# Reordering the transposed loads, the first FFN pass and the output tail of a gated SSM + FFN mix

## The chip, the cores and the metric

The kernel runs on one core of a Trainium2 chip. The metric is the device time of one execution in microseconds (us); lower is better. A core has TensorE (PE in the profile; its weight loads are the row PEld), VectorE (DVE), ScalarE (ACT), GpSimd (POOL) and SyncE (SP), each with an instruction queue of its own that runs in order. Here SP issues nearly all DMAs; ACT issues some at the start.

## The reference

Inputs are bf16; x is 2048 x 448. The result is `g * a + (1 - g) * b`, row by row:

```python
g = sigmoid((x * gate_w).sum(-1, keepdims=True))
# a: a diagonal complex state space model with 448 states
dt = exp(log_dt); Lam_bar = exp(dt * Lam); B_bar = ((Lam_bar - 1) / Lam)[:, None] * (B_re + 1j * B_im)
h[t] = Lam_bar * h[t-1] + B_bar @ x[t]                 # for 2048 steps t
a[t] = 2 * real((C_re + 1j * C_im) @ h[t]) + x[t] * Dskip
# b: a feed-forward network, 448 -> 1792 -> 448
b = silu(x @ w1) @ w2
```

## The kernel before, in words

The program is one function, `gated_mix`. A small class, `Tracker`, keeps for every named buffer who wrote and who read it, and puts semaphore waits in front of each instruction; each engine gets its list in the order in which the function emits it. So the order of the calls in the source is the order of work on every engine, written out by hand.

**Layout.** The 2048 rows are taken as 1024 pairs (`x2` is 1024 x 896: even row, then odd row). `XT` holds x transposed: chunks 0 to 3 are the 448 channels of the even rows, 4 to 7 of the odd rows; three chunks have 128 channels and the last has 64, called the remainder. Halves h = 0, 1 are 512 pairs each. Keys: `XTe00..3` (even, h 0; made by PE transposes), `XTe1` (even, h 1), `XTo0`/`XTr0` and `XTo1`/`XTr1` (odd main chunks / odd remainder of half 0 and 1; all DMA transposes by `ldt`, L221). `XR` holds the remainders once more on the other 64 partitions, copied by `swap_xr` on DVE (L233 for half 1 of the even rows, key `XR1a`; L411 for half 0), so that two matmuls of 64 rows can use the two halves of the PE array side by side. `W1E` is w1, its remainder rows loaded twice, on partitions 0 to 63 (key `W1Ea`) and 64 to 127 (`W1Ez`); `W1Ed` is the larger part of the columns from 896 on. `BT` is B transposed (keys `BT0`, `BT1`; remainders `BT2`, `BT3`), with a DVE copy of the remainder to the other half (L516, key `BTz`) and a packed copy `BR` of 64 re/im columns (L518). `XN` is x as it lies, in two halves `XN0`, `XN1`; `GWB` and `DB` are gate_w and Dskip broadcast to 128 partitions.

**Stages.** `ffn1_first` (L355) and `ffn1(c, ...)` (L326 full chunks, L339 remainders) make the FFN's first product in transposed form for chunk c (c = 0, 1 even halves, 2, 3 odd halves), ACT applies SiLU (L366). `bu(pt, h)` (L660 full chunks, L672 remainders) makes B x for a pair of state blocks; ACT copies it out (L682, L684, L689). Main and remainder matmuls alternate in order (`half`). `scan(pt)` and `scan3()` run the recurrence on DVE: `weigh`, `turn`, `back` and `even` are their steps, `run(gen, n)` emits the next n of them. `gate` (DVE, L585) multiplies `XN` with `GWB`, `gate2` (ACT, L602) sums its rows, `skip` (DVE, L593) multiplies `XN` with `DB`. `ffn2(c, q)` (L629) is the FFN's second product for 128 rows; ACT evicts it with the factor 1 - g (L634). `phases` (POOL, L477 and L479) and `phases2` (DVE, L484) prepare the arguments of the sine tables.

**Output.** 16 tiles of 128 x 448. `yopen` (L828, L830) issues six matmuls of a tile, `yclose` (L841) the two that need the last scan, `yout` (DVE, L851) combines the tile with the gate and the FFN's part into one of 4 buffers of `OT`, and SP stores it (L854). `xg(b)` names places that the gate borrows as scratch: b = 2 is `OT`, b = 3 is `TMPS`.

**Order around the change.** SP issues: x and the weights, `BT0`, `BT1`, `BT2`, `BT3`, `XTo0`, `XTr0`, `XTe1`, `XN0`, `XTo1`, `XTr1`, `XN1`, then W2 and C. PE runs `ffn1_first`, the rest of `ffn1(0)`, `bu(0, 0)`, `bu(3, 0)`, one block of `ffn1(1)`, `bu(0, 1)`, `bu(3, 1)`, the rest of `ffn1(1)`, and on. A block of `ffn1(1)` waits for `XTe1` and `XR1a` before its first matmul; the odd half of `bu(0, 0)` for `XTo0` and `XTr0`, its remainders for all of `BT` and `BTz`; `bu(3, 0)` for `BR`; `bu(0, 1)`, which begins with its remainders, for `XTo1` and `XTr1`.

Of the kernel before, what the change touches and what calls it, by code (L numbers as in the profile page):

```python
# [19 lines left out]
D = 448  # L20
# [126 lines left out]
def gated_mix(nc, A_x, A_Lambda_re, A_Lambda_im, A_B_re, A_B_im, A_C_re, A_C_im, A_log_dt,  # L147
              A_Dskip, B_x, B_w1, B_w2, gate_w, out):
    with ExitStack() as ctx:
        E = ctx.enter_context  # L150
        T = Tracker(nc, ctx)

        def sb(name, shape, dtype):
            return E(nc.sbuf_tensor(name, list(shape), dtype))

        x2 = A_x[0].rearrange("(k i) d -> k (i d)", i=2)
        out2 = out[0].rearrange("(k i) d -> k (i d)", i=2)

# [8 lines left out]
        XR = sb("XR", [128, NK], BF16)  # L167
# [6 lines left out]
        OT = sb("OT", [128, 4, D], BF16)  # L174
# [30 lines left out]
        def xg(b):  # L205
            if b < 2:
                return CO[:, 4 * b:4 * b + 4, :], [f"CO{m}" for m in (range(4) if b == 0 else (1, 4, 5, 6))]
            if b == 2:
                return OT[:, :, :], [f"OT{i}" for i in range(4)]
            v = TMPS[:, :, :].rearrange("p a b -> p (a b)").bitcast(BF16)  # L210
            return v[:, 0:4 * D].rearrange("p (k c) -> p k c", k=4), [f"TMP{i}" for i in range(3)]

        ps = E(nc.psum_tensor("ps", [128, 8, 512], F32))
# [3 lines left out]
        def ld(eng, dst, src, key, group=None):  # L217
            return T.dma(eng, lambda e: e.dma_start(dst, src), writes=[key], group=group)  # L218

        def ldt(dst, src, key, reads=(), group=None, also=()):  # L220
            return T.dma("sp", lambda e: e.dma_start_transpose(dst, src), reads=reads,  # L221
                         writes=[key, *also], group=group)
# [19 lines left out]
        def row(v):  # L242
            return v.rearrange("(o n) -> o n", o=1)
# [5 lines left out]
        for i, eng in enumerate(("sp", "act")):  # L249
            T.dma(eng, lambda e, i=i: e.dma_start(XH[:, 2 * i:2 * i + 2, :], x0[:, 2 * i:2 * i + 2, :]),  # L250
                  writes=COK[i:i + 1])
# [14 lines left out]
        gBT = T.group()  # L266
        for i, src in enumerate((A_B_re, A_B_im)):
            ldt(BT[:, 0:3, i * D:(i + 1) * D], src[:, 0:384], f"BT{i}")
        for i, src in enumerate((A_B_re, A_B_im)):
            ldt(BT[:, 3:4, i * D:(i + 1) * D], src[:, 320:448], f"BT{2 + i}", group=gBT)  # L270

        def ldt_odd(h):
            hs = slice(h * 512, (h + 1) * 512)
            ldt(XT[:, 4:7, hs], x2[hs, 448:832], f"XTo{h}")
            ldt(XT[:, 7:8, hs], x2[hs, 768:896], f"XTr{h}")

        def load_xn(h):
            ld("sp", XN[:, 8 * h * D:8 * (h + 1) * D].rearrange("p (k c) -> p k c", k=4),
               x2[h * 512:(h + 1) * 512, :].rearrange("(k p) c -> p k c", p=128), f"XN{h}")

        for dst, src, key in ((GWB, gate_w, "GW"), (DB, A_Dskip, "DB")):
            ld("act", dst[:, :], row(src).partition_broadcast(128).rearrange("p o n -> p (o n)"), key)
        ldt_odd(0)
        ldt(XT[:, 0:4, 512:1024], x2[512:1024, 0:512], "XTe1")
        load_xn(0)
        ldt_odd(1)
        load_xn(1)
        XC_ALL = ["XC0", "XC1"] + [f"XC3_{q}" for q in range(4)]

        T.op("pool", lambda e: e.memset(ID[:, :], 1.0), writes=["ID"])  # L290
# [4 lines left out]
             writes=["IOTA"])  # L295
# [5 lines left out]


        n_bank = [0]

        def nxt():
            n_bank[0] += 1
            return BANKS[(n_bank[0] - 1) % len(BANKS)]

        half = [False]

        def ffn1_mm(c, fbs):

# [35 lines left out]
        def ffn1_first():  # L348

            banks = [nxt() for _ in range(NFA)]  # L350
            for j in range(4):
                p = slice(0, 128 if j < 3 else 64)

                for fb, bank in enumerate(banks):
                    T.op("pe", lambda pe, fb=fb, bank=bank, j=j, p=p: pe.matmul(  # L355
                        ps[:, bank, :], W1E[p, j, fb * 128:(fb + 1) * 128], XT[p, j, 0:512],
                        start=(j == 0), stop=(j == 3)),
                        reads=[f"W1Ej{j}" if j < 3 else "W1Ea", f"XTe0{j}"], writes=[f"ps{bank}"])
                if j == 0:
                    yield  # L360
            nxt()
            yield list(enumerate(banks))
# [46 lines left out]
        for j in range(4):  # L409
# [9 lines left out]
            reads=["ps7"], writes=["PV"])  # L419
# [12 lines left out]
        def c1(n, pt):  # L432
            i = pc(n)
            return P[:, i, pt:pt + 1]
# [9 lines left out]
        def pact(o, a, f, ra, scale=1.0, bias=0.0):  # L444
# [16 lines left out]
            reads=["f2"] + SGN, writes=["f2s"])  # L461
# [38 lines left out]
        def tmp(m):  # L500
            if m < 4:
# [11 lines left out]
             reads=["li"] + SGN, writes=["lis"])  # L513
# [3 lines left out]
             writes=["BTz"] + BTK[2:4])  # L517
# [293 lines left out]
        n_o = [0]  # L811
# [3 lines left out]
        def state(kt, odd, m):  # L815
            t0 = kt * 128
            return HS[:, m, t0 + H0:t0 + H0 + 128] if odd else VE[:, m, t0:t0 + 128]

        def sk(kt, odd, ms):
            return [f"H{'S' if odd else 'E'}{m}_{kt // 4}" for m in ms]  # L820

        def yopen(kt, odd):
            bank = nxt()

            def mm(pe):
                ins = None
                for m in YA:
                    ins = pe.matmul(ps[:, bank, 0:D], state(kt, odd, m), CO[:, m, :], start=(m == 0), stop=False)  # L828
                tile = 2 * kt + odd
                return pe.matmul(ps[:, bank, 0:D], ID[:, :], XN[:, tile * D:(tile + 1) * D], start=False, stop=False)  # L830
            T.op("pe", mm, reads=sk(kt, odd, YA) + [f"CO{m}" for m in YA] + [f"XD{kt // 2}", "ID"],
                 writes=[f"ps{bank}"])
            return kt, odd, bank

        def yclose(kt, odd, bank):
            tile = 2 * kt + odd

            def mm(pe):
                ins = None
                for m in YB:  # L840
                    ins = pe.matmul(ps[:, bank, 0:D], state(kt, odd, m), CO[:, m, :], start=False, stop=(m == YB[-1]))  # L841
                return ins
            T.op("pe", mm, reads=sk(kt, odd, YB) + [f"CO{m}" for m in YB], writes=[f"ps{bank}"])
            return tile, bank

        def yout(tile, bank):
            kt, odd = tile // 2, tile % 2
            i = n_o[0] % 4
            n_o[0] += 1
            o = OT[:, i, :]  # L850
            T.op("dve", lambda e: e.scalar_tensor_tensor(  # L851
                o, ps[:, bank, 0:D], GT[:, 1, tile:tile + 1], bs(tile), ALU.mult, ALU.add),
                reads=[f"ps{bank}", "GT1", f"BS{tile}"], writes=[f"OT{i}"])
            outs.append(T.dma("sp", lambda e: e.dma_start(  # L854
                out2[kt * 128:(kt + 1) * 128, odd * D:(odd + 1) * D], o),
                reads=[f"OT{i}"], writes=[f"out{tile}"]))
# [7 lines left out]
        def run(g, n=10 ** 9):  # L864
            for _ in range(n):
                if next(g, "end") == "end":
                    break
# [5 lines left out]
        s0, s3, s1, s2 = scan(0), scan3(), scan(1), scan(2, True)  # L873
# [10 lines left out]
        f = ffn1(1)  # L884
# [45 lines left out]
        for q in range(4):  # L930
            ffn2(3, q)
        done = []
        for kt in range(4):
            for odd in (1, 0):
                done.append(yclose(*yopen(kt, odd)))
        run(s2, 1)
        yout(*done.pop(0))
        run(s2, 1)
        while done[2:]:
            yout(*done.pop(0))  # L940
        run(s2, 1)
        while done:
            yout(*done.pop(0))
        opened = [yopen(kt, 1) for kt in range(4, 8)]
        run(s2, 1)
        for kt in range(4, 8):
            opened.append(yopen(kt, 0))
            done.append(yclose(*opened.pop(0)))
        while opened:
            done.append(yclose(*opened.pop(0)))  # L950
        while done:
            yout(*done.pop(0))
        T.wait_all("sp", outs)

        with nc.Block() as block:
# [3 lines left out]
def bass_gated_mix__ssm_conv_s5__dense_activation_silu__prompt_kernel(nc, *args):  # L959
    gated_mix(nc, *args)  # L960
# [28 lines left out]
```

## Time and profile before

| | us |
|---|---|
| median of 3 runs | 151.32 (150.38 to 154.27) |
| the profiled execution | 149.61 |
| its span, first to last instruction | 147.8 |
| PE busy within the span | 139.2 (94%) |
| DVE / ACT / POOL busy | 124.1 / 82.2 / 15.1 |

A timeline row reads: start, duration, engine, line, operation, output<-inputs, shape, how many; a bracket gives the idle time before it and who ended it. "SPq" and "ACTq" are the issuing of DMAs. A row of the DMA view gives the number of issues, the size, and the time from issue to landing. The chain view follows the work that ended last back to the start.

### The profile page before, as it was taken

The page shows a single profiled execution, that of the slowest core. Times are in us where ns is not written, and L with a number is a line of the kernel's source. Part 1 is how long each engine was busy: PE and PEld are TensorE (multiplying, and loading weights), DVE is VectorE, ACT ScalarE, POOL GpSimd, SP SyncE. Part 2 cuts the span into 40 slices and gives each one's busy share as a digit, 9 for nine tenths or more (in the row PEclk, how much of TensorE's full clock was granted, in tenths as well). Part 3 has the DMA queues.
Part 4 walks back from the last instruction along what each step waited for, and adds up shares of the span by engine and source line. Part 5 has one row for each costly group of instructions (what it writes and reads, how often), then busy time and mean ns, then how long its engine had stood idle before and what let it go on. Part 6 is the DMA issues. An engine that isn't in the chain of part 4 may idle for free.

```text
span 147.8 us, 1884 instructions
## 1 busy us (share of the span) xinstructions
PE 139.2 (94%) x715; PEld 63.8 (43%) x715; DVE 124.1 (84%) x164; ACT 82.2 (56%) x130; POOL 15.1 (10%) x20
## 2 busy tenths in 40 slices
PE   6999949799999999999999999999999999999980
PEld 2544313243354543343555343445555555555530
DVE  1673774999999999999999999999999729997372
ACT  1259796868999999995998375471313210000000
POOL 7039990000000000000000000000000000000000
PEclk9999999999999999999999999999999999999997
DMA  4999699999943003003000000000000000211023
GB/s 126 306 248 222 131 164 319 163 381 317 151 102 72 0 0 71 0 0 75 0 0 0 0 0 0 4 0 0 0 0 0 4 0 31 100 55 62 31 93 126
DMA packets 23137, 12.40 MB, mean 84 GB/s; under 512 B 16213, under 2 KB 22617, under 8 KB 23129
## 3 DMA queue, kind: packets, MB, share of 16 engines
q1 hardware_dynamic: 22260, 11.11, 31.8%
q10 hardware_dynamic: 868, 1.18, 3.1%
q8 instruction: 5, 0.08, 0.2%
q14 instruction: 4, 0.02, 0.1%
HBM read 6.26 MB, written 1.84 MB: 55 GB/s over the span
## 4 chain that ended last, share of the span: by engine, by line
PE 62%; ACT 15%; SPq 14%; DMA 5%; issue 2%; DVE 2%; DVEq 0%; ACTq 0%
PE ps L629 21%; PE ps L326 13%; SPq L221 11%; PE ps L828 10%; PE ps L660 8%; DMA XT<-in_A_x_dram 5%; ACT AT L366 3%; PE ps L841 3%; ACT CO L602 3%; PE ps L339 2%; SPq L218 2%; PE ps L830 2%; PE ps L672 2%; DVE OT L851 2%; ACT TMPS L602 2%
## 5 line engine op out<-in xcount | busy, mean ns | idle before, releaser
L629 PE MATMUL ps<-W,AT 128*128 128x448 bf16 x224 | 42.9, 352 | 0.0
L326 PE MATMUL ps<-XT,W1E 128*128 128x512 bf16 x147 | 33.6, 380 | 0.0
L366 ACT ACTIVATE AT<-ps 128x1024 bf16<-128x1024 f32 (+1 forms) x32 | 27.2, 918 | 7.7 <-PE ps L339 7.3
L629 PEld LDWEIGHTS ps<-W,AT 128*128 128x128 bf16 x224 | 21.9, 98 | 20.7 <-ACT AT L366 0.2
L326 PEld LDWEIGHTS ps<-XT,W1E 128*128 128x128 bf16 x147 | 13.7, 98 | 18.9 <-issue 3.0
L660 PE MATMUL ps<-XT,BT 128*128 128x512 bf16 x72 | 16.7, 379 | 1.9 <-issue 1.9
L634 ACT ACTIVATE BT<-ps,GT 128x448 bf16<-128x448 f32 x8 | 5.1, 633 | 15.5 <-PE ps L629 15.5
L851 DVE SCALAR_TENSOR_TENSOR OT<-ps,GT,BT 128x448 bf16<-128x448 f32 x8 | 5.4, 680 | 7.6 <-PE ps L841 7.6
L660 PEld LDWEIGHTS ps<-XT,BT 128*128 128x128 bf16 x72 | 6.7, 98 | 11.1 <-issue 3.7
L730 DVE TENSOR_TENSOR_SCAN G<-P,Q 128x1024 f32<-128x1024 f32 (+1 forms) x6 | 11.3, 1918 | 0.0
L682 ACT ACTIVATE VE<-ps 128x1024 bf16<-128x1024 f32 (+1 forms) x8 | 7.4, 920 | 5.5 <-PE ps L672 4.2
L828 PE MATMUL ps<-CO,HS 128*128 128x448 bf16 x40 | 8.9, 352 | 0.0
L828 PE MATMUL ps<-CO,VE 128*128 128x448 bf16 x40 | 8.9, 352 | 0.0
L696 DVE SCALAR_TENSOR_TENSOR G<-VE,P,HS 128x1024 f32<-128x1024 bf16 (+1 forms) x5 | 7.5, 1494 | 1.6 <-ACT HS L684 1.6
L696 DVE SCALAR_TENSOR_TENSOR HS<-VE,P,G 128x512 bf16<-128x512 bf16 (+1 forms) x10 | 8.1, 856 | 0.2
L684 ACT ACTIVATE HS<-ps 128x1024 bf16<-128x1024 f32 (+1 forms) x8 | 7.4, 921 | 0.8 <-PE ps L660 0.8
L693 DVE TENSOR_TENSOR Q<-G,COS 128x2048 bf16<-128x2048 f32 (+1 forms) x4 | 7.0, 1754 | 0.1
L693 DVE TENSOR_TENSOR Q<-G,SIN 128x2048 bf16<-128x2048 f32 (+1 forms) x4 | 7.0, 1750 | 0.0
L339 PE MATMUL ps<-XT,W1E 64*128 64x512 bf16 x25 | 6.8, 379 | 0.0
L339 PE MATMUL ps<-XR,W1E 64*128 64x512 bf16 x24 | 6.5, 379 | 0.0
L355 PE MATMUL ps<-XT,W1E 128*128 128x512 bf16 (+1 forms) x28 | 6.5, 379 | 0.0
L830 PE MATMUL ps<-XN,ID 128*128 128x448 bf16 x16 | 5.6, 353 | 0.0
(107 smaller groups left out, 181.8 us busy)
## 6 DMA issues: line engine op xcount, KB each, us to landing
XN<-in_A_x_dram SPq DMA_DIRECT2D x2, 896.0 KB, 6.2
out_dram<-OT SPq DMA_DIRECT2D x16, 112.0 KB, 1.7
W<-in_B_w_dram SPq DMA_DIRECT2D x1, 1568.0 KB, 9.0
W1E<-in_B_w_dram ACTq DMA_DIRECT2D x3, 224.0 KB, 6.4
W1E<-in_B_w_dram SPq DMA_DIRECT2D x1, 672.0 KB, 9.2
HS<-HS SPq DMA_DIRECT2D x4, 128.0 KB, 2.4
W1E<-in_B_w_dram SPq DMA_DIRECT2D x2, 224.0 KB, 5.0
CO<-in_A_x_dram SPq DMA_DIRECT2D x1, 256.0 KB, 3.4
```

The costliest lines, as they stand in the source:

```text
L221: return T.dma("sp", lambda e: e.dma_start_transpose(dst, src), reads=reads, writes=[key, *also], group=group)
L326: ins = pe.matmul(ps[:, bank, :], W1E[:, j, fb * 128:(fb + 1) * 128], XT[:, x0 + j, hs], start=(j == 0 and not rf), stop=(j == 2 and rf))
L339: ins = pe.matmul(ps[:, bank, :], W1E[p, 3, fb * 128:(fb + 1) * 128], x, start=rf, stop=not rf)
L366: T.op("act", lambda e: e.activation(a[:, fb:fb + n, :], ps[:, bank:bank + n, :], AF.Silu), reads=[f"ps{bank + i}" for i in range(n)], wri ...
L629: ins = pe.matmul(ps[:, bank, 0:D], a[:, fb, q * 128:(q + 1) * 128], W2[:, fb, :], start=(fb == 0), stop=(fb == NFB - 1))
L660: ins = pe.matmul(ps[:, bank, :], bt(slice(0, 128), j, m), XT[:, 4 * odd + j, hs], start=(j == 0 and not rf), stop=(j == 2 and rf))
L693: T.op("dve", lambda e: e.tensor_tensor(o, a, b, op), reads=reads, writes=writes)
L696: T.op("dve", lambda e: e.scalar_tensor_tensor(o, a, s, b, ALU.mult, ALU.add), reads=reads, writes=writes)
L730: T.op("dve", lambda e, c=c, init=init: e.tensor_tensor_scan(G[:, c, w], rb, Q1[:, c, w], init, ALU.mult, ALU.add), reads=[f"Q1{c}", "rr", ...
L828: ins = pe.matmul(ps[:, bank, 0:D], state(kt, odd, m), CO[:, m, :], start=(m == 0), stop=False)
L830: return pe.matmul(ps[:, bank, 0:D], ID[:, :], XN[:, tile * D:(tile + 1) * D], start=False, stop=False)
L851: T.op("dve", lambda e: e.scalar_tensor_tensor(o, ps[:, bank, 0:D], GT[:, 1, tile:tile + 1], bs(tile), ALU.mult, ALU.add), reads=[f"ps{ban ...
```

## The change

Five edits:

1. **DMA order on SP.** `XTo0` and `XTr0` go ahead of `BT2` and `BT3`; `XTo1` and `XTr1` go ahead of `XN0`; `XN0` and `XN1` come last. The loads of `GWB` and `DB` move from ACT's queue to SP's, between `XTr1` and `XN0`.
2. **`ffn1_first`.** In its last pass (the remainders) every second matmul uses the upper copy: `W1E[64:128]` and `XR` in place of `W1E[0:64]` and `XT`.
3. **Order of the tail.** `turn` of the last scan step comes ahead of the first `yout`, and the first eight tiles are put out two, four and two at a time between `turn`, `back` and `even`. The last eight tiles keep one tile open ahead: open, open, close, open, close, and so on.
4. **Store buffers.** `yout` goes round 8 buffers: 4 in `OT` and 4 in the place of `TMPS`.
5. `half` is set a few lines earlier in the source.

```diff
         for i, src in enumerate((A_B_re, A_B_im)):
             ldt(BT[:, 0:3, i * D:(i + 1) * D], src[:, 0:384], f"BT{i}")
-        for i, src in enumerate((A_B_re, A_B_im)):
-            ldt(BT[:, 3:4, i * D:(i + 1) * D], src[:, 320:448], f"BT{2 + i}", group=gBT)
...
+        ldt_odd(0)
+        for i, src in enumerate((A_B_re, A_B_im)):
+            ldt(BT[:, 3:4, i * D:(i + 1) * D], src[:, 320:448], f"BT{2 + i}", group=gBT)
+        ldt(XT[:, 0:4, 512:1024], x2[512:1024, 0:512], "XTe1")
+        ldt_odd(1)
         for dst, src, key in ((GWB, gate_w, "GW"), (DB, A_Dskip, "DB")):
-            ld("act", dst[:, :], row(src).partition_broadcast(128).rearrange("p o n -> p (o n)"), key)
-        ldt_odd(0)
-        ldt(XT[:, 0:4, 512:1024], x2[512:1024, 0:512], "XTe1")
+            ld("sp", dst[:, :], row(src).partition_broadcast(128).rearrange("p o n -> p (o n)"), key)
         load_xn(0)
-        ldt_odd(1)
         load_xn(1)
...
             for j in range(4):
-                p = slice(0, 128 if j < 3 else 64)
                 for fb, bank in enumerate(banks):
...
+                    up = j == 3 and fb % 2 == 1
+                    p = slice(64, 128) if up else slice(0, 128 if j < 3 else 64)
+                    x = XR[p, 0:512] if up else XT[p, j, 0:512]
...
         def yout(tile, bank):
-            i = n_o[0] % 4
+            i = n_o[0] % 8
             n_o[0] += 1
-            o = OT[:, i, :]
+            o = OT[:, i, :] if i < 4 else xg(3)[0][:, i - 4, :]
...
         for kt in range(4):
             for odd in (1, 0):
                 done.append(yclose(*yopen(kt, odd)))
+        run(s2, 2)
+        flush(2)
         run(s2, 1)
-        yout(*done.pop(0))
+        flush(4)
         run(s2, 1)
-        while done[2:]:
-            yout(*done.pop(0))
-        run(s2, 1)
-        while done:
-            yout(*done.pop(0))
-        opened = [yopen(kt, 1) for kt in range(4, 8)]
-        run(s2, 1)
-        for kt in range(4, 8):
-            opened.append(yopen(kt, 0))
-            done.append(yclose(*opened.pop(0)))
+        flush(8)
+        tiles = [(kt, 1) for kt in range(4, 8)] + [(kt, 0) for kt in range(4, 8)]
+        opened = [yopen(*tiles.pop(0)), yopen(*tiles.pop(0))]
         while opened:
             done.append(yclose(*opened.pop(0)))
-        while done:
-            yout(*done.pop(0))
+            if tiles:
+                opened.append(yopen(*tiles.pop(0)))
+        flush(8)
```

`flush(n)` calls `yout` for up to n closed tiles.

More of the change, by code (lines that the diff above doesn't have):

```diff
@@ L208, in xg @@
             if b == 2:
-                return OT[:, :, :], [f"OT{i}" for i in range(4)]
+                return OT[:, 0:4, :], [f"OT{i}" for i in range(4)]
             v = TMPS[:, :, :].rearrange("p a b -> p (a b)").bitcast(BF16)
@@ L303, in gated_mix @@
         n_bank = [0]
+        half = [False]
         def nxt():
@@ L307, in nxt @@
             return BANKS[(n_bank[0] - 1) % len(BANKS)]
-        half = [False]
         def ffn1_mm(c, fbs):
@@ L351, in ffn1_first @@
             for j in range(4):
-                p = slice(0, 128 if j < 3 else 64)
                 for fb, bank in enumerate(banks):
[L355 to L358, printed above, removed]
+                    up = j == 3 and fb % 2 == 1
+                    p = slice(64, 128) if up else slice(0, 128 if j < 3 else 64)
+                    x = XR[p, 0:512] if up else XT[p, j, 0:512]
+                    T.op("pe", lambda pe, fb=fb, bank=bank, j=j, p=p, x=x: pe.matmul(
+                        ps[:, bank, :], W1E[p, j, fb * 128:(fb + 1) * 128], x, start=(j == 0), stop=(j == 3)),
+                        reads=[f"W1Ej{j}" if j < 3 else "W1Ez" if up else "W1Ea", "XR0a" if up else f"XTe0{j}"],
+                        writes=[f"ps{bank}"])
                 if j == 0:
@@ L847, in yout @@
             kt, odd = tile // 2, tile % 2
-            i = n_o[0] % 4
+            i = n_o[0] % 8
             n_o[0] += 1
-            o = OT[:, i, :]
+            o = OT[:, i, :] if i < 4 else xg(3)[0][:, i - 4, :]
+            extra = xg(3)[1] + ["CT4", "CT5", "CT6"] if n_o[0] == 5 else []
             T.op("dve", lambda e: e.scalar_tensor_tensor(
                 o, ps[:, bank, 0:D], GT[:, 1, tile:tile + 1], bs(tile), ALU.mult, ALU.add),
-                reads=[f"ps{bank}", "GT1", f"BS{tile}"], writes=[f"OT{i}"])
+                reads=[f"ps{bank}", "GT1", f"BS{tile}"], writes=[f"OT{i}"] + extra)
             outs.append(T.dma("sp", lambda e: e.dma_start(
@@ L932, in gated_mix, with flush @@
         done = []
+        def flush(n):
+            for _ in range(n):
+                if done:
+                    yout(*done.pop(0))
         for kt in range(4):
```

## The prediction

> **What bounds the kernel now.** I read the page first, then TensorE's timeline for the places where it stands still, then the queue that feeds it there, then the end.
>
> ```profile
> PE 139.2 (94%) x715; PEld 63.8 (43%) x715; DVE 124.1 (84%) x164; ACT 82.2 (56%) x130; POOL 15.1 (10%) x20
> ```
>
> TensorE is busy for 139.2 us, 94% of the span, so a gain must come out of the other 6%, 8.6 us, or out of shorter TensorE work. Its timeline, where it stops or where an edit touches it:
>
> ```profile
> 18.16 1.46 PE L660 MATMUL ps<-XT,BT 128*128 128x512 bf16 x6
> 21.53 1.46 PE L660 MATMUL ps<-XT,BT 128*128 128x512 bf16 x6 [1.91 <-issue]
> 23.36 0.38 PE L672 MATMUL ps<-XT,BR 64*128 64x512 bf16 x2
> 24.98 2.75 PE L326 MATMUL ps<-XT,W1E 128*128 128x512 bf16 x12
> 27.89 0.38 PE L339 MATMUL ps<-XR,W1E 64*128 64x512 bf16 x1
> 29.18 0.61 PE L672 MATMUL ps<-XT,BT 64*128 64x512 bf16 x4 [0.91 <-DMA XT<-in_A_x_dram]
> 41.80 8.49 PE L629 MATMUL ps<-W,AT 128*128 128x448 bf16 x44
> 55.98 0.61 PE L672 MATMUL ps<-XT,BT 64*128 64x512 bf16 x4 [0.29 <-ACT IOTA L634]
> ```
>
> The stops are the odd half of `bu(0, 0)` at 21.53, `bu(0, 1)` at 29.18, and 0.29 us at 55.98. The bracket at 21.53 names nobody; the queue does. Here is SP's issuing, first from the chain (start, duration): `BT2` at 12.93, `BT3` after it, then `XTo0`, `XTr0`, `XTe1`, `XN0`; from 21.43 `XTo1`, which the chain follows to its landing. The last row is from SP's timeline, `XTo1` and `XTr1` together.
>
> ```profile
> 12.93 1.26 SPq L221
> 15.53 1.51 SPq L221
> 17.08 1.26 SPq L221
> 18.39 1.67 SPq L221
> 20.10 1.29 SPq L218
> 21.43 7.14 DMA XT<-in_A_x_dram
> 21.43 5.47 SPq L221 DMA_TRANSPOSE XT<-in_A_x_dram  x2
> ```
>
> The DMA view for single issues gives the time to landing, in order `W1Ed`; `W1Ez`, `GWB`, `DB`; `BT3`; `XTr0`; `XTr1`; `XN0`; W2.
>
> ```profile
> W1E<-in_B_w_dram SPq DMA_DIRECT2D x1, 672.0 KB, 9.2
> W1E<-in_B_w_dram ACTq DMA_DIRECT2D x1, 224.0 KB, 8.2
> GWB<-in_gate_w_dram ACTq DMA_DIRECT2D x1, 112.0 KB, 8.7
> DB<-in_A_Dskip_dram ACTq DMA_DIRECT2D x1, 112.0 KB, 8.4
> BT<-in_A_B_im_dram SPq DMA_TRANSPOSE x1, 2.8
> XT<-in_A_x_dram SPq DMA_TRANSPOSE x1, 4.4
> XT<-in_A_x_dram SPq DMA_TRANSPOSE x1, 5.1
> XN<-in_A_x_dram SPq DMA_DIRECT2D x1, 896.0 KB, 7.2
> W<-in_B_w_dram SPq DMA_DIRECT2D x1, 1568.0 KB, 9.0
> ```
>
> `XTr0`, issued at 17.08, lands at 17.08 + 4.4 = 21.5: that is the first stop. `XTr1`, issued in the second half of the 5.47 us, lands just ahead of 29.18: the second. So early on the order of transposes on one queue bounds TensorE. The end:
>
> ```profile
> 119.00:142.00 23.00, 23.00 (x123) 11.91 (x122) 17.01 (x24) 0.63 (x1) 0.00 (x0) 1.00 0.15 50
> 120.87 0.68 DVE L851 SCALAR_TENSOR_TENSOR OT<-ps,GT,BT 128x448 bf16<-128x448 f32 x1 [3.66 <-PE ps L841]
> 141.86 1.68 PE L841 MATMUL ps<-CO,VE 128*128 128x448 bf16 x8
> 142.66 1.86 DVE L851 SCALAR_TENSOR_TENSOR OT<-ps,GT,FP 128x448 bf16<-128x448 f32 x3
> 144.92 0.68 DVE L851 SCALAR_TENSOR_TENSOR OT<-ps,GT,FP 128x448 bf16<-128x448 f32 x1 [0.40 <-DVE OT L851]
> ```
>
> In the first row (stretch, then TensorE's, the weight loads' and DVE's busy time) TensorE has no gap from 119 to 142 while DVE works 17.0 of 23.0 us. TensorE ends at 143.54, and the four closes at the very end come in one burst (8 matmuls), so DVE finishes 2.06 us behind it, at 145.60, the last 0.40 waiting for a store buffer. The span ends 2.2 after that, with the last store.
>
> **The change, part by part.**
>
> *First FFN pass.* A paired block of the chain costs 0.97 us for eight remainders, and twelve full matmuls take 2.75 (the row at 24.98), 0.23 each:
>
> ```profile
> 61.87 0.97 PE ps L339 x8
> 12.54 2.27 PEld L326 LDWEIGHTS ps<-XT,W1E 128*128 128x128 bf16 x12 [0.42 <-DMA W1E<-in_B_w_dram]
> ```
>
> Seven remainders one by one are 7 x 0.23 = 1.6; one alone and three pairs are 0.23 + 3 x 0.24 = 0.95. At most 0.65 is saved. Against it: the upper copy `W1Ez`, issued at 3.27, lands at 3.27 + 8.2 = 11.5, and `W1Ed`, issued at 2.86, at 12.1, and the first weight load of the next block is the one that waits for it (12.54). So 0 to 0.65 early in `ffn1(0)`. It counts as nothing, because `ffn1(1)` will wait below for something else; had TensorE no such wait, it would be worth its 0.65.
>
> *Odd x earlier.* `XTo0` and `XTr0` take the slots of `BT2` and `BT3`, `XTr0` the one near 14.4: landing 14.4 + 4.4 = 18.8, ahead of 19.5 where the even half ends. The stop of 1.91 goes. What is late next: `BT3`, now in the slot of 17.08. Moving `GWB` and `DB` off ACT's queue helps all of SP's early transfers by s. Bounds for s: 0, if SP's own weights hold its queue, and 1.4, the time from `W1Ez`'s landing (11.5) to `DB`'s (4.48 + 8.4 = 12.9), which ACT's queue spent on these two. I take 0.7, half, since two queues shared the engines. Then `BT3` goes out at 16.4 and lands after 2.8 (its own row) to 4.4 (the row of that slot): 19.2 to 20.8. I take 20.0.
>
> DVE stands behind it, in order:
>
> ```profile
> 18.87 0.39 DVE L516 COPY BT<-BT 64x896 bf16<-64x896 bf16 x1
> 19.40 1.00 DVE L518 COPY BR<-BT 128x512 bf16<-128x512 bf16 x1
> 20.32 1.21 DVE L484 SCALAR_TENSOR_TENSOR FP<-G,FP 128x1024 f32<-128x1024 f32 x1
> 22.46 1.23 DVE L484 SCALAR_TENSOR_TENSOR FP<-G,FP 128x1024 f32<-128x1024 f32 x1 [0.94 <-POOL G L479]
> 23.72 0.29 DVE L233 COPY XR<-XT 64x512 bf16<-64x512 bf16 x1
> 20.34 2.09 POOL L479 TENSOR_SCALAR G<-FP 128x1024 f32<-128x1024 f32 x1
> ```
>
> L516 now waits for `BT3`, and behind it on DVE are `BR`, two `phases2` and the swap that makes `XR1a`, for which `ffn1(1)` waits. From `BT3`'s landing that is 0.53 + 0.92 + 1.14 + 1.26 + 0.29 = 4.14 by starts; but not before 24.01, its end today, since POOL's last phase is not moved. So `XR1a` stands at 24.01 to 24.94, at 24.14 for 20.0. `bu(0, 0)` (remainders after 20.4) and `bu(3, 0)` (`BR` at 21.5, then 24.98 - 23.36 = 1.62) are done by 23.2. `XTe1` keeps its slot, 18.39, and lands after 5.1 by 23.5. So `ffn1(1)` starts at about 24.25 in place of 24.98: gain 0.7, bounds 0 and 0.92.
>
> The Trainium skill bears on the 1.00 us of `BR`. "SBUF — State Buffer", section "SBUF: two separate sides", says that the port pair of DVE and GpSimd is an exclusive lock held for a whole instruction. The trace agrees: L518 needed 1.00 for 512 columns, L516 only 0.39 for 896, and L484 at 22.46 starts just when POOL's 2.09 us are over. By that rule a late `BT3` lets POOL run ahead, `BR` shrinks towards 0.39, but POOL's own phase then falls between DVE's copies; by my estimate from these rows `XR1a` comes near 24.4, and the sum would be 0.2 to 0.3 less.
>
> *The second half of odd x.* `XTo1` takes `XN0`'s slot: 20.10 in place of 21.43, less s. So `XTr1` lands at least 1.33 earlier, at 27.8 or before, and without `XN0`'s 896 KB ahead sooner still. TensorE, at 24.25, reaches `bu(0, 1)` at 27.4, which then starts right behind the last remainder (today 27.89 + 0.23 = 28.12) and not at 29.18: gain 1.06. Bounds 0.7 (s = 0, slowest) and 1.06.
>
> *Natural x, gate_w and Dskip later.* Two issues come to SP ahead of `XN0`, the longer 0.91 long on ACT:
>
> ```profile
> 4.48 0.91 ACTq L218 DMA_DIRECT2D DB<-in_A_Dskip_dram  x1
> 37.40 0.57 ACT L602 ACTIVATE CO<-CO 128x448 bf16<-128x448 bf16 x1
> ```
>
> Today `XTr1` is issued by 26.90, then by 25.6 at the latest, so `XN0` goes out by 27.4 and lands after 7.2 by 34.6, against 27.3 today. Behind it on DVE stands L585, the gate's product, and behind that the Dskip products and every scan. ACT sums that product at 37.40, 35.6 after the gain, so ACT doesn't wait. DVE itself can lose 7.3: it idles 6.0 in the row of the tail and 1.8 just ahead of it (3.66 less 120.87 - 119), 7.8 together. Price 0; without this cover, one for one. W2 follows by 30.0 (two `XN` issues of 1.29) and lands after 9.0 by 39.0; `ffn2(0)`, its first reader, is at 41.80, 40.0 after the gain. The Trainium skill, "DMA: Bandwidth & Descriptors", section "Issuing engines are not separate DMA queues", says that all queues run on the same engines and that another queue saves only issuing time. By it the 224 KB are not saved but put behind odd x, and the sum stays; no run here shows it yet.
>
> *Tail.* `turn` moves into DVE's 3.66 us idle. Its steps then end some 4 us sooner than TensorE needs them; the eight buffers remove the 0.40. The order open, close brings the closes 1.51 apart but for the last two, 0.38 apart. The last `yout` starts 0.60 (the step of the three in 1.86) after one that starts at TensorE's end - 0.34: it ends 0.94 behind TensorE, not 2.06. Gain 1.12; bounds 0.4 (the buffer wait alone) and 1.2. Nothing is computed more or less, and the 0.29 at 55.98 stays, as TensorE and ACT move together there.
>
> **Sum.** 0.7 + 1.06 + 1.12 = 2.9 us: the profiled execution's 149.61 would be 146.7, its span 144.9. That execution lies 1.7 under the median of the runs, 151.32, on which I put the forecast: 148.4.
>
> **Rivals.** *BT3 later than 21.* For: transposes in that region took up to 5.1, and s may be 0. Against: its own 2.8. Then `ffn1(1)` gains nothing and the sum is 1.06 + 1.12 = 2.2: 149.1.
>
> *The early gain doesn't arrive.* ACT, for whose L634 TensorE already waits 0.29 at 55.98, may take it if the gate's product comes later than 35.6. For: `XN0` landing at 34.6 leaves DVE 1.0 for it. Against: 34.6 adds every delay to the latest. Only the tail is left: 150.2.
>
> *Slower.* One mechanism, at L516 on DVE: `BT3`'s landing blocks everything DVE has, `XR1a` included. Each us after 20.8 costs one us; the early gain of 1.06 is gone at 21.9 and the tail's at 23.0, and from there the kernel is slower. That takes a latency of 6.6 us; 7.14 stands in the chain for `XTo1` behind `XN0`, which would give 151.32 + 0.5 = 151.8. Against: what stood before that one, 896 KB of `XN0`, does not stand before `BT3`.
>
> **How the numbers follow.** Chances: forecast 0.62, late `BT3` 0.18, tail only 0.14, slower 0.06. The forecast's own bounds are 0 + 0.7 + 0.4 = 1.1 and 0.92 + 1.06 + 1.2 = 3.2. The range runs from the profiled execution less 3.2, 146.4, as runs may be like that one, to the lowest of these sums and the tail-only case, both 150.2. Two per cent, 3.0 us, is about what a measurement of this kernel can tell from no change; the forecast lies just inside it, so of its 0.62 about 0.40 would measure as faster. Within is the rest of it, the next two cases (0.32) and half of the slower one, 0.57 together; 0.03 is slower.
>
> **What would show it.** Right: no stop at the odd half of `bu(0, 0)`; a new wait of `ffn1(1)` for DVE's L233 near 24.2; no wait for XT at `bu(0, 1)`; DVE waiting for a DMA at L516; TensorE's end near 141.8 and the last `yout` one microsecond behind it. Wrong: L516 after 21, a gap on ACT ahead of L602, DVE in place of TensorE as releaser in the tail, or `bu(0, 1)` still waiting.

## The result, and the profile after

The changed kernel takes 147.0 us (median of four runs, 146.49 to 147.32) against 151.37 for the kernel before, measured beside it (150.38 to 154.27). The ratio is 0.973, 95% interval 0.967 to 0.979: 4.1 us faster. The forecast was 148.4, range 146.4 to 150.2. A second set of six runs gave a ratio of 0.968 (0.962 to 0.973). The ratios leave out executions over 1.5% above the fastest of their kernel, so the medians beside them can differ a little more or less.

The profiled execution after is 147.32 us with a span of 145.6, 2.3 us below the profiled one of before (149.61). The gap between the medians is larger, and that difference is a main point below. The first row of the page and TensorE's timeline, for the blocks shown of before, with the first FFN1 pass in front:

```profile
PE 139.0 (95%) x715; PEld 63.7 (44%) x715; DVE 124.1 (85%) x164; ACT 82.1 (56%) x130; POOL 15.2 (10%) x20
```

```profile
12.47 0.39 PE L356 MATMUL ps<-XR,W1E 64*128 64x512 bf16 x1 [0.56 <-DMA W1E<-in_B_w_dram]
...
18.84 2.75 PE L661 MATMUL ps<-XT,BT 128*128 128x512 bf16 x12
...
24.80 2.75 PE L326 MATMUL ps<-XT,W1E 128*128 128x512 bf16 x12 [1.05 <-issue]
...
27.92 0.59 PE L673 MATMUL ps<-XT,BT 64*128 64x512 bf16 x4
...
54.73 0.61 PE L673 MATMUL ps<-XT,BT 64*128 64x512 bf16 x4 [0.30 <-ACT IOTA L635]
```

TensorE's work is the same (139.0 after 139.2, 715 matmuls). The twelve full matmuls of `bu(0, 0)` now run as one block: the stop of 1.91 is gone. `ffn1(1)` has a new wait of 1.05, whose bracket names nobody. `bu(0, 1)` starts without one at 27.92, 1.26 ahead of 29.18, and that 1.26 is kept: the wait of 0.30 stands at 54.73 where it stood at 55.98. In the first pass the upper weights, `W1Ez`, are now waited for (0.56).

SP's issuing after, from its timeline (start, duration). The two transposes at 12.79 are `XTo0` and `XTr0`; then `BT2`, `BT3`; the three at 18.07 are `XTe1`, `XTo1`, `XTr1`; natural x comes after `GWB` and `DB`. Behind it, from the DMA view for single issues, the time from issue to landing of `BT3`, of `XN0` and of W2 (`W`):

```profile
12.79 2.65 SPq L221 DMA_TRANSPOSE XT<-in_A_x_dram  x2
15.47 1.26 SPq L221 DMA_TRANSPOSE BT<-in_A_B_re_dram  x1
16.77 1.26 SPq L221 DMA_TRANSPOSE BT<-in_A_B_im_dram  x1
18.07 5.37 SPq L221 DMA_TRANSPOSE XT<-in_A_x_dram  x3
23.48 0.58 SPq L218 DMA_DIRECT2D GWB<-in_gate_w_dram  x1
24.11 0.43 SPq L218 DMA_DIRECT2D DB<-in_A_Dskip_dram  x1
24.58 1.00 SPq L218 DMA_DIRECT2D XN<-in_A_x_dram  x2
```

```profile
BT<-in_A_B_im_dram SPq DMA_TRANSPOSE x1, 2.8
XN<-in_A_x_dram SPq DMA_DIRECT2D x1, 896.0 KB, 7.4
W<-in_B_w_dram SPq DMA_DIRECT2D x1, 1568.0 KB, 14.3
```

`BT3` lands at 16.77 + 2.8 = 19.6, `XN0` at 24.58 + 7.4 = 32.0. W2 is issued at 25.62 and lands at 39.9; `ffn2(0)`, its first reader, starts at 40.54. DVE and POOL, from their timelines, show what that does:

```profile
19.64 0.39 DVE L517 COPY BT<-BT 64x896 bf16<-64x896 bf16 x1 [0.15 <-DMA BT<-in_A_B_im_dram]
20.16 0.92 DVE L519 COPY BR<-BT 128x512 bf16<-128x512 bf16 x1
...
23.15 1.23 DVE L485 SCALAR_TENSOR_TENSOR FP<-G,FP 128x1024 f32<-128x1024 f32 x1 [0.94 <-POOL G L480]
24.41 0.29 DVE L233 COPY XR<-XT 64x512 bf16<-64x512 bf16 x1
...
32.05 2.22 DVE L586 TENSOR_TENSOR CO<-XN,GWB 128x1792 bf16<-128x1792 bf16 x2 [2.80 <-DMA XN<-in_A_x_dram]
21.03 2.09 POOL L480 TENSOR_SCALAR G<-FP 128x1024 f32<-128x1024 f32 x1
```

`XR1a` is ready at 24.41 + 0.29 = 24.70, 0.10 ahead of `ffn1(1)`. Natural x makes DVE wait 2.80, as foreseen. The gate's product ends at 34.27, and ACT sums it at once behind its own work:

```profile
36.14 0.57 ACT L603 ACTIVATE CO<-CO 128x448 bf16<-128x448 bf16 x1
```

The end, from the stretch view and the timelines of TensorE and DVE:

```profile
119.00:142.00 23.00, 23.00 (x124) 11.84 (x121) 19.43 (x29) 0.00 (x0) 0.00 (x0) 1.00 0.19 65
119.61 0.69 DVE L694 TENSOR_TENSOR Q<-HS,COS 128x1024 bf16<-128x1024 bf16 x1
141.36 0.92 PE L842 MATMUL ps<-CO,VE 128*128 128x448 bf16 x4
141.94 1.28 DVE L853 SCALAR_TENSOR_TENSOR TMPS<-ps,GT,FP 128x448 bf16<-128x448 f32 x2 [0.83 <-PE ps L842]
```

TensorE still has no gap from 119 to 142; DVE, set back by its wait for natural x, has more of its work left for this stretch (19.43 us in place of 17.01) and does it without delaying TensorE. The last closes are two tiles, not four. TensorE ends at 142.28, DVE at 143.22, 0.94 behind, with no wait for a buffer.

### The profile page after: what moved, and what is told of

Its sections match the earlier page's. It is cut to its first block, busy times and chain, and to the rows that moved or that the text cites. A ratio compares the mean times of both kernels' runs of the same rounds, so it can differ in the third digit from the quotient of the medians.

```text
span 145.6 us, 1882 instructions
## 1 busy us (share of the span) xinstructions
PE 139.0 (95%) x715; PEld 63.7 (44%) x715; DVE 124.1 (85%) x164; ACT 82.1 (56%) x130; POOL 15.2 (10%) x20
## 4 chain that ended last, share of the span: by engine, by line
PE 73%; ACT 15%; DMA 6%; ACTq 2%; issue 1%; DVEq 1%; DVE 0%
PE ps L630 22%; PE ps L326 18%; PE ps L661 11%; PE ps L829 10%; DMA W1E<-in_B_w_dram 6%; PE ps L842 4%; PE ps L339 3%; ACT AT L367 3%; ACT CO L603 3%; PE ps L673 2%; PE ps L831 2%; ACT OT L603 2%; ACT TMPS L603 2%; ACT IOTA L635 2%; ACTq L218 1%
## 5 line engine op out<-in xcount | busy, mean ns | idle before, releaser
L829 PEld LDWEIGHTS ps<-CO,VE 128*128 128x128 bf16 x40 | 3.9, 98 | 3.7
## 6 DMA issues: line engine op xcount, KB each, us to landing
W<-in_B_w_dram SPq DMA_DIRECT2D x1, 1568.0 KB, 14.3
```

## The experiments

The theory: the gain is the tail's (about 1.1 us) and, for the rest, loads in an order that lets odd x land ahead of its use. The rivals: that TensorE's clock, and not the order, makes the difference; and that one of the smaller edits (pairing, the place of B's remainders, the place of natural x, the queue of gate_w and Dskip) carries it. The first four kernels ran together on one chip, the next four on another, the last four on a third; each set has its own runs of the kernel before.

**The kernel before, unchanged**, is the measure of scatter.

> The kernel before, unchanged, as a control: what the medians can tell, and a second profile of it. Both theories: ratio 1.00. Theory A (the prediction's sum: order of odd x and the tail, 2.2 to 2.9 us): the profile repeats the first one, span 147.8 within 0.3, stops of TensorE of about 1.9 at the odd half of bu(0, 0) and 0.9 at bu(0, 1). Theory B (the profiled execution of before was a short one; the runs' median lies 1.7 us above it because the early transposes land later in most executions): the span is 149 or more and the two stops together are 4 us or more in place of 2.8.

Median 151.76 (150.21 to 153.8), ratio 0.989 (0.982 to 0.997) for the same program: in this set one per cent means nothing. Its profile is of a longer execution (152.82), and both stops are longer than in the first profile, 2.56 and 1.81 in place of 1.91 and 0.91:

```profile
22.03 1.45 PE L660 MATMUL ps<-XT,BT 128*128 128x512 bf16 x6 [2.56 <-issue]
...
30.58 0.61 PE L672 MATMUL ps<-XT,BT 64*128 64x512 bf16 x4 [1.81 <-DMA XT<-in_A_x_dram]
```

`bu(0, 1)` stands 1.40 later than in the first profile. Behind it TensorE's granted clock was 0.50 from 32 to 34.

**The DMA order alone**, on the kernel before: the change's edits of lines 266 to 290, nothing else. In short, the order of the issues (not lines of the source):

```
-        BT2, BT3; GWB, DB on ACT; ldt_odd(0); XTe1; load_xn(0); ldt_odd(1); load_xn(1)
+        ldt_odd(0); BT2, BT3; XTe1; ldt_odd(1); GWB, DB on SP; load_xn(0); load_xn(1)
```

> Before with the new DMA order alone (odd x ahead of B's remainders and of natural x, gate_w and Dskip on SP's queue). Theory A: 1.1 to 1.8 us faster than before, ratio 0.988 to 0.993. Theory B: it takes the scatter of the early landings off TensorE's path too and gains 3 us, ratio 0.98.

148.23 us, ratio 0.975 (0.968 to 0.981). TensorE's timeline, then DVE's and POOL's:

```profile
22.50 0.61 PE L673 MATMUL ps<-XT,BT 64*128 64x512 bf16 x4 [1.17 <-DVE BT L517]
...
25.56 2.75 PE L327 MATMUL ps<-XT,W1E 128*128 128x512 bf16 x12 [0.83 <-issue]
...
28.68 0.59 PE L673 MATMUL ps<-XT,BT 64*128 64x512 bf16 x4
22.06 0.39 DVE L517 COPY BT<-BT 64x896 bf16<-64x896 bf16 x1 [2.79 <-DMA BT<-in_A_B_im_dram]
22.58 0.29 DVE L519 COPY BR<-BT 128x512 bf16<-128x512 bf16 x1
20.56 1.04 POOL L480 TENSOR_SCALAR G<-FP 128x1024 f32<-128x1024 f32 x1
```

Here `BT3` came at 22.06, past the 21 from which the prediction saw the gain at `ffn1(1)` gone, and this profiled run, 149.49, was the longest of its six. The loss stands at the place named, and `bu(0, 1)` still has no wait. The ratio is measured against the set whose control gave 0.989 for the same program, so it may flatter the order by up to one per cent.

**The tail alone**, on the kernel before: eight store buffers, `flush`, one tile open ahead (the change's edits at line 209 and from 848 on).

```
-            i = n_o[0] % 4
+            i = n_o[0] % 8
...
-        opened = [yopen(kt, 1) for kt in range(4, 8)]
+        opened = [yopen(*tiles.pop(0)), yopen(*tiles.pop(0))]
```

> Before with the new tail alone (order of turn and the stores, one tile open ahead, 8 store buffers). Theories A and B: 1.1 us faster, ratio 0.9925, the last DVE instruction 0.94 us behind TensorE's end in place of 2.06. A rival that gives the tail the missing 1.5 us (stores that land late in most executions hold the 4 buffers): 2.5 us faster, ratio 0.983.

Median 152.7 (149.23 to 153.59), ratio 0.986 (0.975 to 0.996): with the control's 0.989 beside it, inconclusive, since the scatter of the old loading order is larger than the tail. The trace of its profiled run (153.59) has the step that was meant: TensorE ends at 148.61 and DVE at 149.55, 0.94 behind. It also has the longest wait of `bu(0, 1)` of all the profiles:

```profile
32.89 1.04 PE L672 MATMUL ps<-XT,BT 64*128 64x512 bf16 x4 [3.38 <-DMA XT<-in_A_x_dram]
```

The old tail on the new order, below, gives the tail's price.

**The pairing alone**, on the kernel before.

```
+                    up = j == 3 and fb % 2 == 1
+                    p = slice(64, 128) if up else slice(0, 128 if j < 3 else 64)
+                    x = XR[p, 0:512] if up else XT[p, j, 0:512]
...
```

> Before with the paired remainders of the first FFN1 pass alone. Theory A: nothing, ratio 1.00, because the odd half of bu(0, 0) waits for XTr0 all the same. Rival: 0.65 us faster (0.996), if the first pass is on the path. A third: up to 0.5 slower, where the upper copy of the remainder weights lands after the lower one and stops the pass.

Ratio 0.993 (0.986 to 0.999), not told apart from the control. The first timeline row is its price, a wait for `W1Ez`; the others are the old stops, and the stretch is TensorE's clock between them (1.00 would be full speed):

```profile
11.71 0.39 PE L356 MATMUL ps<-XR,W1E 64*128 64x512 bf16 x1 [0.31 <-DMA W1E<-in_B_w_dram]
...
22.10 2.30 PE L661 MATMUL ps<-XT,BT 128*128 128x512 bf16 x6 [2.44 <-issue]
...
31.45 0.61 PE L673 MATMUL ps<-XT,BT 64*128 64x512 bf16 x4 [1.02 <-DMA XT<-in_A_x_dram]
23.00:25.00 2.00, 2.00 (x8) 0.49 (x8) 1.10 (x2) 0.00 (x0) 0.00 (x0) 0.50 1.03 243
```

**The changed kernel again**, as the measure for the next three.

> The changed kernel, unchanged, beside the next three on the same chip. Theory C (the clock): in the kernel before, TensorE's early stops bring on a stretch of 3.4 us at half clock in many executions; the new order leaves stops too short for that. Expects ratio 0.97 and a clock of 0.995 or more in every run of this kernel, against 0.983 to 1.0 for the kernel before. Theory A (the prediction's sum alone): ratio 0.98, and a clock that differs as often as before's.

146.62 us (146.37 to 147.61), ratio 0.968 (0.962 to 0.973). Its profiled execution is its longest run, 147.61; TensorE's timeline has the same picture as the first profile after:

```profile
25.00 2.75 PE L326 MATMUL ps<-XT,W1E 128*128 128x512 bf16 x12 [1.55 <-issue]
...
28.13 0.59 PE L673 MATMUL ps<-XT,BT 64*128 64x512 bf16 x4
```

**The changed kernel with the old tail**: the edit of the tail taken back.

```
-        tiles = [(kt, 1) for kt in range(4, 8)] + [(kt, 0) for kt in range(4, 8)]
...
+        opened = [yopen(kt, 1) for kt in range(4, 8)]
```

> The changed kernel with the old tail (4 store buffers, the old order of yopen, yclose and yout). Theory A's price of the tail: 1.1 us slower than the changed kernel, span 1.1 longer at the same end of TensorE, the last DVE instruction 2.06 us behind TensorE in place of 0.94. Rival (the two runs of one part each left the tail unclear): the order of odd x has it all and this kernel is as fast as the changed one within 0.3 us.

148.09 us, ratio 0.977 (0.972 to 0.982): the tail is worth 148.09 - 146.62 = 1.47 us. The old burst is back, and with it the buffer wait (TensorE's and DVE's timelines):

```profile
140.12 1.68 PE L842 MATMUL ps<-CO,VE 128*128 128x448 bf16 x8
143.18 0.68 DVE L852 SCALAR_TENSOR_TENSOR OT<-ps,GT,FP 128x448 bf16<-128x448 f32 x1 [0.40 <-DVE OT L852]
```

TensorE ends at 141.80 and DVE at 143.86, 2.06 behind as in before, so the trace gives 2.06 - 0.94 = 1.12; no row places the other 0.35. `ffn1(1)` starts earlier in this profile than in the two of the changed kernel, whose code ahead of the tail is the same:

```profile
24.31 2.75 PE L326 MATMUL ps<-XT,W1E 128*128 128x512 bf16 x12 [0.83 <-issue]
```

**The changed kernel without the pairing.**

```
-                    up = j == 3 and fb % 2 == 1
...
+                p = slice(0, 128 if j < 3 else 64)
...
```

> The changed kernel without the paired remainders in the first FFN1 pass. Theory A: within 0.3 us of the changed kernel, since the first block of ffn1(1) waits for the copy that makes XR1a in both, near 24.7. Rival: 0.65 us slower (the pass is on the path) or 0.5 faster (the wait for the upper copy of the remainder weights, 0.56 us in the changed kernel's profile, is gone).

146.7 us, ratio 0.969 (0.964 to 0.974): 0.1 us from the changed kernel, nothing. The seven remainders run one by one again, and `ffn1(1)` starts no later than in the profile of the full change:

```profile
21.63 0.60 PE L672 MATMUL ps<-XT,BT 64*128 64x512 bf16 x4 [0.64 <-DVE BT L516]
...
24.69 2.75 PE L326 MATMUL ps<-XT,W1E 128*128 128x512 bf16 x12 [0.83 <-issue]
```

**The changed kernel with `XR1a` made earlier**, to take away the new wait at `ffn1(1)`.

```
         phases2(1)
+        swap_xr("dve", 1, 0)
         phases2(2)
-        swap_xr("dve", 1, 0)
```

> The changed kernel with the copy that makes XR1a moved on DVE's queue ahead of the second of the two phases2 in front of it, which waits for POOL. If that copy is what the first block of ffn1(1) waits for (1.05 us in the changed kernel's profile), the block starts when bu(3, 0) ends, the wait is below 0.3 us, and the kernel is 0.7 to 1.0 us faster than the changed kernel. Rival: XTe1's landing (23.0 in the changed kernel) is what ends the wait, and no more than 0.3 us comes of it, or the next wait, for XTr1 at bu(0, 1), takes it back.

146.46 us, ratio 0.967 (0.962 to 0.972), against 0.968: by the times, nothing. The trace does what was meant:

```profile
23.27 2.75 PE L326 MATMUL ps<-XT,W1E 128*128 128x512 bf16 x12
...
26.93 0.61 PE L673 MATMUL ps<-XT,BT 64*128 64x512 bf16 x4 [0.37 <-ACT VE L690]
```

`ffn1(1)` starts 1.5 earlier than in the changed kernel's profile, so the copy behind `XR1a` is what it waited for there, and ACT takes back 0.37. W2 lands at 26.55 + 12.9 = 39.45 in this run, and `ffn2(0)` starts at 39.58: little more could be had here before W2 stops it. This run (146.36) is no shorter than three of the changed kernel's six (146.37, 146.38, 146.38), whose profiled one was its longest. So the wait of 1.05 to 1.55 may belong to the two profiled executions and not to the usual one; those shorter runs left no trace, and this stays open.

**The kernel before with TensorE kept busy**: dummy matmuls in the two stops, which compute nothing that is used. It parts the clock from the waits.

```
+                    if odd and pt == 0 and h == 0:
+                        warm(9)
...
+        warm(5, 2)
         bu(0, 1)
```

> The kernel before with idle time filled: 9 matmuls on zeros between the two halves of bu(0, 0) and 5 ahead of bu(0, 1), into a free bank, where TensorE waits for XTr0 and XTr1. They compute nothing that is used. Theory C (long stops bring on 3.4 us at half clock): clock 0.993 or more in every run, no half-clock stretch before 140, and the median 0.7 to 1.5 us below before's. Rival (the clock falls for reasons of its own, or the half-clock stretch falls into waits anyway): clocks spread like before's, from 0.983, and ratio 1.00.

Ratio 1.002 (0.997 to 1.006): no gain by this measure. The medians of all runs are 151.2 against 151.9, and 0.7 is the least that the theory of the clock expected. The granted clock was 0.994 to 1.0 in ten of twelve runs, while 10 of the 17 runs of before in that set lay below 0.99. With the clock kept, `bu(0, 1)` still waits for odd x:

```profile
22.19 1.46 PE L662 MATMUL ps<-XT,BT 128*128 128x512 bf16 x6
...
31.41 0.61 PE L674 MATMUL ps<-XT,BT 64*128 64x512 bf16 x4 [1.29 <-DMA XT<-in_A_x_dram]
```

The second half of odd x lands just ahead of 31.41 here, where the prediction's execution had it ahead of 29.18. At the first stop the dummies themselves stand until 22.19, so this kernel doesn't show how long that wait would have been.

The runs of before settle the rival better. In this set its ten runs with a clock below 0.99 have a median of 152.75 and the other seven one of 150.94: a lost clock goes with 1.8 us. But in the changed kernel's set the five runs of before with a clock of 0.993 to 0.998 have a median of 150.87, still 4.2 above the changed kernel's 146.62. So the clock lengthens many runs of before, and it is not what carries the gain.

The last three put back one place of the new order each, and ran with the last one here as the nearest to the changed kernel.

**gate_w and Dskip back on ACT's queue, ahead of odd x.**

```
+            ld("act", dst[:, :], row(src).partition_broadcast(128).rearrange("p o n -> p (o n)"), key)
         ldt_odd(0)
...
         ldt_odd(1)
...
-            ld("sp", dst[:, :], row(src).partition_broadcast(128).rearrange("p o n -> p (o n)"), key)
```

> The changed kernel with the loads of GWB and DB back on ACT's queue at the start. The term s of the prediction (0 to 1.4, taken 0.7): the profiles since show the issuing of BT1 ending at 12.2 to 12.9 with these loads late and at 12.9 to 14.8 with them early. If s is 1.1: BT1's issue ends near 13.5, BT3 lands after 20, XTe1 near 24, and the kernel is 0.5 to 1.0 us slower than the changed one, 147.2 to 147.6. If s is near 0: the same time within 0.2.

148.03 us, ratio 0.974 (0.968 to 0.981). SP's timeline, DVE's and TensorE's:

```profile
7.30 6.81 SPq L221 DMA_TRANSPOSE BT<-in_A_B_im_dram  x1
25.41 0.29 DVE L233 COPY XR<-XT 64x512 bf16<-64x512 bf16 x1 [1.22 <-DMA XT<-in_A_x_dram]
12.72 0.39 PE L356 MATMUL ps<-XR,W1E 64*128 64x512 bf16 x1 [1.38 <-DMA W1E<-in_B_w_dram]
...
25.80 2.75 PE L326 MATMUL ps<-XT,W1E 128*128 128x512 bf16 x12 [1.81 <-DMA XT<-in_A_x_dram]
```

`BT1`'s issuing ends at 14.11; in the changed kernel the next issue starts at 12.79, here at 14.15. SP's next transposes stand 1.4 us later, and `ffn1(1)` waits for `XTe1` itself. It is not this pair alone: in the six profiles with the two loads early, `BT1`'s issuing ends at 12.89 to 14.76, in the eight with them late at 11.96 to 12.86.

**Natural x's first half back ahead of the second half of odd x.**

```
+        load_xn(0)
         ldt_odd(1)
...
-        load_xn(0)
```

> The changed kernel with XN0 back ahead of XTo1. Theory: XTr1 lands at 28 to 30 again, bu(0, 1) stops 1 to 2 us for it, and the kernel is 1 to 2 us slower than the changed one (147.7 to 148.7), more where the stop brings on the half clock. DVE's wait for XN0 (2.8 to 4.1 us in the profiles) goes and pays nothing. Rival: DVE's wait is on the path, and the kernel is as fast as the changed one or faster.

147.69 us (147.18 to 148.39 in five runs, 150.86 in one), ratio 0.972 (0.966 to 0.978). SP's issue of `XTo1` slips behind `XN0`'s (start, duration), and TensorE waits for `XTr1` again:

```profile
20.30 0.59 SPq L218 DMA_DIRECT2D XN<-in_A_x_dram  x1
20.94 5.79 SPq L221 DMA_TRANSPOSE XT<-in_A_x_dram  x2
28.91 0.61 PE L673 MATMUL ps<-XT,BT 64*128 64x512 bf16 x4 [1.32 <-DMA XT<-in_A_x_dram]
```

**B's remainders back ahead of the first half of odd x.**

```
+        for i, src in enumerate((A_B_re, A_B_im)):
+            ldt(BT[:, 3:4, i * D:(i + 1) * D], src[:, 320:448], f"BT{2 + i}", group=gBT)
         ldt_odd(0)
```

> The changed kernel with BT2 and BT3 back ahead of XTo0 and XTr0. Theory: XTr0 lands near 21, the odd half of bu(0, 0) stops about 1.3 us, but bu(3, 0) then ends at 24.3 to 24.6 in place of 23.5, just where ffn1(1) waits for XR1a anyway, so no more than 0.4 us is lost (146.6 to 147.0). Rival: the whole 1.3 us is lost (147.9).

146.95 us, ratio 0.968 (0.962 to 0.974): the changed kernel's. The stop at the odd half comes back with 0.80, and `ffn1(1)` waits 0.9 less for it:

```profile
20.28 1.46 PE L661 MATMUL ps<-XT,BT 128*128 128x512 bf16 x6 [0.80 <-issue]
...
24.05 2.75 PE L326 MATMUL ps<-XT,W1E 128*128 128x512 bf16 x12 [0.16 <-issue]
```

The stop ahead of `ffn1(1)` and the one inside `bu(0, 0)` are one and the same slack, shifted. Against this kernel, on the same chip, gate_w's place is worth 148.03 - 146.95 = 1.1 us and natural x's 0.7, or 0.9 and 0.6 by the ratios. The intervals overlap, so these are sizes and not exact prices; five of the six runs with gate_w early are longer than all six of this kernel.

## Why the prediction was right, and what it mis-sized

**Tail: right, by its steps.** The burst of four became two, the last `yout` ends 0.94 behind TensorE as worked out, TensorE's end (142.28, forecast near 141.8) is later by the 0.5 that the early part fell short. The old tail costs 1.47 by medians, 1.12 by the trace.

**First FFN1 pass at nothing: right.** `W1Ez` now costs a wait of 0.56, what the pairs save goes into it, and `ffn1(1)` waits for `XR1a` anyway. Without the pairing the time is the same.

**Natural x, gate_w, Dskip later at no price: right.** The gate's product starts 32.05, under the 34.6 allowed; DVE waits 2.80 for it and pays out of its slack in the tail (19.43 busy of 23.0). ACT sums it at 36.14, where 35.6 was forecast, and without a gap in front. One term held by luck: W2 was to land after 9.0, its latency in the kernel before, and it took 14.3 (11.0 to 15.0 in the nine profiles with the new order or most of it, 9.0 to 9.4 in the five of the old). It went out at 25.62, well ahead of the 30.0 allowed, and so landed 0.6 ahead of its first reader.

**`bu(0, 1)` without a wait: right.** 27.92 after 27.4 forecast.

**`ffn1(1)` at 24.25: 0.55 too early.** The step that failed is the limit of `XR1a`. I put it on `BT3` at 20.0, and `BT3` came sooner, at 19.6, by two errors that nearly cancel: it went out at 16.77 for 16.4 and landed after 2.8, the shortest time considered. POOL, which I had taken as unmoved, started its last phase 0.69 later (21.03, not 20.34) and released DVE's last `phases2`, whose start moved from 22.46 to 23.15. The trace follows most of this back: POOL's first phase already starts 0.60 later (10.43 for 9.83); it waits for DVE, DVE for TensorE's small products (8.21 for 7.62), and the transposes of x ahead of those began at 4.58 for 4.23, behind a wait for the load of x. In all the profiles that first phase of POOL starts at 9.58 to 10.67, and the two of the changed kernel are among the late ones; no experiment was made on what moves the landing of x. With POOL's first phase at 9.94, in the run with the old tail, `ffn1(1)` started at 24.31, near the forecast. So the profiled pair shows 1.26 for the early part, not 1.76.

The lock rule of the Trainium skill ("SBUF — State Buffer", "SBUF: two separate sides") agrees with the traces here: `BR` took 0.92 beside POOL's phase, and 0.29 in the run of the order alone, where POOL had ended at 21.60 before it began. That run also shows the chain behind a late `BT3` to be shorter than the 4.14 that I added up from rows beside a busy POOL: `XR1a` was ready at 25.46, 3.40 after 22.06. Of the two values that the prediction had for `XR1a`, 24.14 and 24.4 by the rule, the 24.70 of the changed kernel is nearer to the second, but POOL's late start set it. The start of L484 at 22.46, which I read as a sign of the lock, is none: its bracket names POOL's result `G`, for which it waits in any case.

**s, the lift of SP's transposes: inside its bounds, but not a constant.** 0.7 was taken, between 0 and 1.4. In the profiled pair it was only 0.14 (SP's next issue at 12.79 for 12.93); with gate_w and Dskip back on ACT's queue `BT1`'s issuing ended 1.3 later and the kernel took about 1.0 us more. The Trainium skill, "DMA: Bandwidth & Descriptors", section "Issuing engines are not separate DMA queues", says that all queues share the same engines; the run agrees, as 224 KB on ACT's queue hold up SP's transposes. The change moved these loads to another queue and to a later time at once, and no run parts the two.

**The base: the term that made the forecast 1.4 us too high.** The sum of 2.9 was made on an execution of 149.61 and then taken off the median, 151.32, as if the 1.7 between them lay elsewhere and would stay. As far as the profiles show, it lay largely in the very waits that the change removes. The profiled execution of before, 149.61, was shorter than all 43 runs of the same kernel in the comparisons (149.93 to 155.75). Two longer executions with the old order, of the pairing alone (152.22) and of the filled kernel (152.26), have `bu(0, 1)` at 31.45 and 31.41, still waiting for odd x: 2.2 to 2.3 us behind the 29.18 of the first profile, and so most of the 2.6 by which they are longer. The two other profiles of the old order, of the kernel before again and of the tail alone, have it at 30.58 and 32.89. The five stand in the order in which `BT1`'s issuing ended: 12.89 in the first profile, then 13.43, 13.84, 14.02 and 14.76. So the first profile had little of the delay that the change removes. With the new order `bu(0, 1)` stands at 27.92, 28.13, 28.68 (the order alone) and 26.93 (`XR1a` earlier). That the median execution of before waits in the same place is inferred from these, as only single executions are profiled. Part of the 1.7 is the clock, but the smaller part: the runs of before that kept it still have medians of 150.87 and 150.94, 1.3 above the first profile. Taken off its own execution the sum gives 146.7, and the changed kernel measured 147.0 and 146.6. That this fits so well is in part luck, as the profiled pair gained 2.3 and not 2.9; the profiled execution after was the longest of its four. The new order took the scatter away as well: ten runs of the changed kernel lie between 146.37 and 147.61.

**Where the 4.1 us went, by parts.** Tail 1.1 to 1.5; gate_w and Dskip later 0.9 to 1.1; natural x later 0.6 to 0.7; B's remainders and the pairing about nothing. These add to 2.6 to 3.3, of 4.1 by the first comparison and 4.9 by the second (ratio 0.968). What is left, one to two microseconds, no single step places: each was put back alone, with the others still there to cover for it, and intervals of half a per cent on each side don't allow a finer split. That it belongs to the order as a whole is shown: without the new tail the changed kernel still had 0.977 (0.972 to 0.982), about 3.5 us, and the pairing is worth nothing. The order put on the kernel before by itself gave 0.975, in the set whose control gave 0.989.

## What to carry to other kernels

Ask of a profiled execution whether it is a usual one before a sum is taken off the median: where the run-to-run difference lies in waits that the change removes, the sum belongs to that execution. Here the changed kernel landed near the short execution less the sum, not at the median less the sum. Loads that are not needed soon can cost time from another queue too, as the 224 KB on ACT's did here beside SP's urgent transposes, so try them behind these in time. An engine with slack later (DVE's 7.8 us here) can pay for a late operand early, as long as no other engine has to wait for its results in between. And look at the load behind the ones that were moved: W2's took 14.3 us in place of 9.0 and came 0.6 us ahead of its use.

## What was not expected of the hardware

In the run of the pairing a stop of 2.44 us was followed by half speed: the stretch 23 to 25 has a clock of 0.50, and six matmuls took 2.30 instead of 1.46. The 1.91 of the first profile brought no such stretch there. Nor is the length of the one stop enough to tell: in the second profile of before the six matmuls behind a stop of 2.56 ran at full speed (1.45), and the half clock came only behind the next stop, of 1.81. The changed kernel's stops (at most 1.55 in its traces) never did this: its clock was 0.999 or 1.0 in all ten runs. The Trainium skill, "TensorE: Matmul & The Clock Gate", section "Why this matters for your kernels", asks for no gaps over about 3 us. The stop of 3.38 in the run of the tail alone was followed by half clock (0.50 from 33 to 35), and here less than that was enough once. The runs of before that kept their clock, still 4.2 us behind the changed kernel, show that this is not what the gain comes from.
